# Packed attention and FFN on one core: FFN tiles of 384 tokens over pairs of batches, with the first pair in float32, in place of tiles of 288 tokens of one batch

## The chip, the cores and the metric

The kernel runs on one core of one Trainium2 chip. The metric is the device time of one execution in microseconds; lower is better. The kernel before took 830.7, 831.4 and 833.71 us in three runs, so the median is 831.4 us.

## What is computed

The reference, cut to what matters. There are 8 batches, 8 heads of 64 dimensions, 576 tokens per batch and 32 pack queries per head; the model width is 512 and d_ff is 2048.

```python
def sm_attn(qq, kk, vv):
    s = scale * qq @ kk.T
    a = exp(s - max(s)); a = a / (sum(a) + 1e-9)
    return a @ vv

p_packed = sm_attn(p, k, v)              # 32 x 64 per head
out = sm_attn(q, p_packed, p_packed)     # 576 x 64 per head
x = out, all heads side by side          # 4608 tokens x 512
h = x @ w_in                             # 4608 x 2048
g = maximum(h, 0) + alpha * minimum(h, 0)
y = g @ w_out                            # 4608 x 512
```

q, k, v, p and alpha are float32; w_in and w_out arrive as float64.

## The kernel before, in words

**Precision.** Most matmuls run in fp32r, a type whose matmul is one pass. To keep float32 accuracy an operand is split in two parts: hi is the operand cast to fp32r, lo is what is left (operand minus hi), and a product is three matmuls, hi·hi, hi·lo and lo·hi. A few parts run as plain float32 matmuls instead, without a split; the profile shows such a matmul as two records.

**Weights.** The float64 weights come in as raw 64-bit words, in blocks of 128 rows by 512 columns: 16 blocks of w_in and 16 of w_out. `convert` makes float32 of a block (ScalarE L117 and L119, VectorE L120, L123, L127 and L131) and splits it (ScalarE L133, VectorE L134). The split w_out stays on chip (`wo0` to `wo15`). The split w_in is used for the first batch at once and written to DRAM (`w_split`), from where later batches read it again.

**Attention.** The heads are handled in four pairs. `attention(b, tp)` does two pairs of one batch: scores of p against k, a softmax, transposes of its weights, a product with v (this gives the packed result), then scores of q against the packed result and a second softmax, whose weights end as `a_h` and `a_l` (split) or `a_f` (float32). The attention of batches 0 and 1 runs in float32 (`exact`): its scores are copied from PSUM to SBUF (L202, L204) before the softmax reads them. In later batches the score's hi and lo parts are added on VectorE (L211).

**Folding the packed result into w_in.** The second product of the attention, weights times packed result, is never made by itself. `packed_w` multiplies the packed result of a batch by w_in, three matmuls of 512 columns per block (L435 to L437), which gives `pw`; the FFN's first matmul is then attention weights times `pw`.

**The FFN.** It goes in steps. A step is one tile of 288 tokens (half a batch) and one block of 128 of the 2048 columns of d_ff; there are 16 tiles and 16 blocks, so 256 steps. `first(k, f)` makes h for the step in PSUM tile `ps_h`: six fp32r matmuls of 288 columns (L480 to L482, twice), or for batch 0 two float32 matmuls (L468). The leaky relu is `neg` on ScalarE (L486) and a multiply-add on VectorE (L487); then h is split into `gh` (ScalarE, L492) and `gl` (VectorE, L493). `second(k, f)` adds the step to four accumulators of 128 output columns each, with three matmuls of 288 columns per accumulator (L505 to L507). `split_pw` (L456, L458) splits `pw` for a tile before its steps need it.

**The order of the work.** One loop at the end of the program walks the 256 steps; at each step it also advances generators that do the rest, by the start steps in `plan`. The first 32 steps interleave the two tiles of batch 0 in blocks of four f, since the weights of a block come one by one; their partial sums are kept in `part` (L511, L518). The conversions of w_in and w_out advance one each in every second step of that stretch. `second` runs two steps behind `first`. From this program a scheduler writes a fixed order of instructions for each engine. SyncE issues all transfers in one queue, in its own order.

Of the kernel before, what the change touches and what calls it, by code (L numbers as in the profile page):

```python
# [15 lines left out]

# [12 lines left out]
def pack_attention_ffn_kernel(  # L29
# [13 lines left out]

# [19 lines left out]
    NG = S // 32  # L63

    const = ctx.enter_context(tc.tile_pool(name="const", bufs=1))
    xin = ctx.enter_context(tc.tile_pool(name="xin", bufs=3))
# [13 lines left out]

    w_split = dram.tile([NJ, NP, P, 2, 512], F32, name="w_split")


# [10 lines left out]
    s1f = const.tile([P, NP, 64], F32, name="s1f")  # L94
    p2f = const.tile([P, NP, 64], F32, name="p2f")
    pt0 = const.tile([P, NP, 2, 2, 64], F32R, name="pt0", tag=f"wo{NF - 1}")
    for t in (s1f, p2f, fv(s1), fv(p2), fv(pt0)):
        nc.gpsimd.memset(t, 0.0)
    wo_t = {}

    XF = 1

    def convert(src, raw, place):

# [10 lines left out]
        mag = xin.tile([P, 512], F32, name="mag", tag="xh")  # L115
        bits = mag.bitcast(U32)
        nc.scalar.activation(out=mag, in_=up, func=AF.Abs)  # L117
        low = xin.tile([P, 512], U32, name="low", tag="xl")
# [13 lines left out]
        hi, lo = place()  # L132
        nc.scalar.copy(out=hi, in_=mag)  # L133
        nc.vector.tensor_tensor(out=lo, in0=mag, in1=fv(hi), op=ALU.subtract)  # L134

    def new_raw(f=0):

        if f in left:
            left.remove(f)
            n = f  # L140
        elif f == NF - 1:
            n = f
        else:
            n = left.pop(0)
            left.append(n)
        return const.tile([P, 512], U64, name=f"wraw{n}", tag=f"wo{n}")

    SPARE = 4
    left = list(range(NF - 1 - SPARE, NF - 1))

    def load_w_out(f):
        def place():
            wo_t[f] = const.tile([P, 2, DM], F32R, name=f"wo{f}", tag=f"wo{f}")
            return wo_t[f][:, 0, :], wo_t[f][:, 1, :]

        raw = new_raw(f)
        convert(w_out[f * P : (f + 1) * P, :], raw, place)


    def load_x(src, b, pr):  # L160
        if b == 0 and (src is kT or pr == NP - 1):
            n = pr if src is kT else 2 * NP
            raw = const.tile([P, S], F32, name=f"xraw{n}", tag=f"wo{n}")
        else:
            raw = xin.tile([P, S], F32, name="xraw", tag="xraw", bufs=3)
        nc.sync.dma_start(out=raw, in_=src[b, pr])
        return raw
# [8 lines left out]
    def load_v(b, pr):  # L176
        if b == 0:
            raw = const.tile([P, KT, P], F32, name=f"vraw{pr}", tag=f"wo{NP + pr}")
        else:
            raw = vin.tile([P, KT, P], F32, name="vraw", tag="vraw")  # L180
        nc.gpsimd.memset(raw[: KT * P - S, KT - 1, :], 0.0)
        nc.sync.dma_start(
            out=raw[:, : KT - 1, :],
            in_=v[b, pr, : (KT - 1) * P].rearrange("(kt kp) d -> kp kt d", kp=P),
        )
        nc.sync.dma_start(out=raw[KT * P - S :, KT - 1, :], in_=v[b, pr, (KT - 1) * P :])
        return raw

    def scores(b, pr, st, x, dst, exact):

# [24 lines left out]
    def new_a(b):  # L215
        a_h = at.tile([P, 2, S], F32R, name="a_h", tag="a_h")
        a_l = at.tile([P, 2, S], F32R, name="a_l", tag="a_l", bufs=4)
        result[b] = (a_h, a_l)

    def attention(b, tp, exact=False):  # L220

# [48 lines left out]
        def split_v(i):  # L270
            if exact:
                return vraw[i]
# [361 lines left out]
```

## Time and profile before

| what | value |
|---|---|
| median of the three runs | 831.4 us |
| span of the profiled execution | 829.4 us |
| median minus span | 2.0 us |
| PE (matmul) busy | 784.3 us |
| VectorE (DVE) busy | 613.7 us |
| ScalarE (ACT) busy | 486.3 us |
| GpSimd (POOL) busy | 196.6 us |
| bytes moved | 97.97 MB |

The profile is of one execution. Its page gives the span, from the first to the last instruction; no time of the same execution beside the span is given, so the difference of 2.0 us between the runs' median and the span stands for what lies around it. PE is TensorE's matmul side and PEld its weight loads, which overlap. The matmuls are pipelined, so a record of a matmul lasts longer than the distance to the next one's start; it is the distance between starts that adds up to time. In a row of a group of instructions stand the line, the engine, the operation, output and input tiles, their shapes, the count; then busy time and the mean of one in ns; then the idle time of the engine before them and what ended it. In rows of windows stand the window, its length, and the busy time and count of each engine in the order PE, PEld, DVE, ACT, POOL, then the granted TensorE clock, the share of the DMA engines' time and GB/s.

### The profile page before, as it was taken

What the parts mean: (1) busy time and instruction counts of PE and PEld (TensorE: products, weight loads), DVE (VectorE), ACT (ScalarE), POOL (GpSimd) and SP (SyncE); (2) the same over time, 40 slices, a digit from 0 to 9 for tenths busy, and PEclk for the clock granted to TensorE, in tenths of its full rate; (3) what the DMA queues carried; (4) which work ended last, traced back from release to release, by engine and by line L of the source; (5) the groups of instructions that cost most, each with busy time, mean ns of one, the idle gap of its engine ahead of it and who ended that gap; (6) DMA issues with size and microseconds to landing.
All of it is one profiled execution on the core that took longest, in us unless ns stands there. A gap on an engine that the chain in (4) does not pass through costs nothing.

```text
span 829.4 us, 14959 instructions
## 1 busy us (share of the span) xinstructions
PE 784.3 (95%) x5384; PEld 730.6 (88%) x5384; DVE 613.7 (74%) x1311; ACT 486.3 (59%) x1141; POOL 196.6 (24%) x195
## 2 busy tenths in 40 slices
PE   5589989999999999999999999899999999999997
PEld 3348777798899989998999999889999999999997
DVE  4999999975777657889886587986955566666663
ACT  5778857756666775655567665655655433333332
POOL 2000012337666302353361024533210000000000
PEclk9779999999999999999999999999999999999999
DMA  9876846455523661322227532300252000000000
GB/s 304 279 249 224 291 166 232 151 180 168 202 90 109 223 203 33 101 59 72 61 76 247 186 87 58 100 15 16 88 196 91 14 30 2 29 1 29 5 27 29
DMA packets 55386, 97.97 MB, mean 118 GB/s; under 512 B 5136, under 2 KB 32784, under 8 KB 55312
## 3 DMA queue, kind: packets, MB, share of 16 engines
q1 hardware_dynamic: 55312, 97.02, 36.1%
q8 instruction: 42, 0.69, 0.3%
q14 instruction: 32, 0.26, 0.1%
HBM read 79.18 MB, written 17.83 MB: 117 GB/s over the span
## 4 chain that ended last, share of the span: by engine, by line
PE 73%; DVE 15%; DMA 5%; ACT 4%; issue 2%; POOL 0%; SPq 0%; ACTq 0%; DVEq 0%
PE acc L505 14%; PE acc L506 13%; PE acc L507 13%; PE ps_h L480 6%; PE ps_h L482 6%; PE ps_h L481 6%; PE ps_h L468 2%; PE ps_m L435 2%; DMA outT<-ot 1%; PE ps_m L436 1%; PE ps_m L437 1%; PE ps_m L316 1%; DVE ps_h L487 1%; DVE pwl L458 1%; DMA w<-w_split 1%
## 5 line engine op out<-in xcount | busy, mean ns | idle before, releaser
L505 PE MATMUL acc<-gh,wo 128*128 128x288 f32 x1024 | 288.6, 301 | 10.9 <-ACT gh L492 9.9
L506 PE MATMUL acc<-gh,wo 128*128 128x288 f32 x1024 | 282.6, 294 | 0.0
L505 PEld LDWEIGHTS acc<-gh,wo 128*128 128x128 f32 x1024 | 192.2, 188 | 22.3 <-ACT gh L492 15.2
L507 PE MATMUL acc<-gl,wo 128*128 128x288 f32 x1024 | 205.3, 300 | 0.0
L506 PEld LDWEIGHTS acc<-gh,wo 128*128 128x128 f32 x1024 | 192.3, 188 | 1.6
L492 ACT CAST gh<-ps_h 128x288 fp32r<-128x288 f32 x256 | 102.2, 400 | 124.1 <-DVE ps_h L487 114.8
L486 ACT ACTIVATE neg<-ps_h 128x288 f32<-128x288 f32 x256 | 105.4, 412 | 111.8 <-PE ps_h L482 102.6
L493 DVE TENSOR_TENSOR gl<-ps_h,gh 128x288 fp32r<-128x288 f32 x256 | 115.4, 452 | 73.4 <-ACT gh L492 72.4
L487 DVE SCALAR_TENSOR_TENSOR ps_h<-neg,nal,ps_h 128x288 f32<-128x288 f32 x256 | 132.0, 516 | 42.6 <-ACT neg L486 41.3
L507 PEld LDWEIGHTS acc<-gl,wo 128*128 128x128 f32 x1024 | 159.0, 188 | 3.7 <-issue 0.4
L480 PE MATMUL ps_h<-a_h,pwh 128*128 128x288 f32 x448 | 133.9, 299 | 1.1 <-DVE gl L493 0.6
L482 PE MATMUL ps_h<-a_h,pwl 128*128 128x288 f32 x448 | 131.8, 295 | 0.6 <-POOL pwl L458 0.6
L481 PE MATMUL ps_h<-a_l,pwh 128*128 128x288 f32 x448 | 131.9, 295 | 0.0
L173 POOL TENSOR_TENSOR xl<-xraw,xh 128x576 fp32r<-128x576 f32 x48 | 70.2, 1463 | 148.6 <-ACT xh L172 143.8
L480 PEld LDWEIGHTS ps_h<-a_h,pwh 128*128 128x128 f32 x448 | 84.1, 188 | 3.5 <-DVE gl L493 1.9
L482 PEld LDWEIGHTS ps_h<-a_h,pwl 128*128 128x128 f32 x448 | 83.9, 188 | 1.4 <-POOL pwl L458 1.1
L481 PEld LDWEIGHTS ps_h<-a_l,pwh 128*128 128x128 f32 x448 | 84.1, 188 | 0.4
L458 DVE TENSOR_TENSOR pwl<-pw,pwh 128x512 fp32r<-128x512 f32 x96 | 73.9, 770 | 7.1 <-PE ps_h L482 1.2
L456 DVE CAST pwh<-pw 128x512 fp32r<-128x512 f32 x112 | 56.0, 503 | 30.1 <-PE ps_h L481 28.6
L443 ACT COPY pw<-ps_m 64x512 f32<-64x512 f32 x112 | 65.0, 580 | 16.7 <-PE ps_m L437 12.7
L275 POOL TENSOR_TENSOR vs<-vraw,vs 128x640 fp32r<-128x640 f32 x24 | 38.6, 1609 | 42.7 <-ACT vs L274 42.2
L210 ACT COPY lo<-ps_m 64x288 f32<-64x288 f32 x96 | 37.8, 396 | 11.3 <-PE ps_m L208 9.8
(114 smaller groups left out, 1018.4 us busy)
## 6 DMA issues: line engine op xcount, KB each, us to landing
w<-w_split SPq DMA_DIRECT2D x64, 512.0 KB, 4.3
xraw<-in_kT SPq DMA_DIRECT2D x32, 288.0 KB, 2.9
xraw<-in_qT SPq DMA_DIRECT2D x32, 288.0 KB, 2.9
outT<-ot SPq DMA_DIRECT2D x64, 144.0 KB, 1.8
vraw<-in_v SPq DMA_DIRECT2D x32, 256.0 KB, 3.0
wraw<-in_w_out SPq DMA_DIRECT2D x16, 512.0 KB, 4.5
wraw<-in_w_in SPq DMA_DIRECT2D x16, 512.0 KB, 4.4
w_split<-w SPq DMA_DIRECT2D x16, 512.0 KB, 4.0
```

The source lines that it names most:

```text
L173: nc.gpsimd.tensor_tensor(out=xl, in0=raw, in1=fv(xh), op=ALU.subtract)
L458: eng.tensor_tensor(out=tl, in0=src, in1=fv(th), op=ALU.subtract)
L480: nc.tensor.matmul(ps[:, :HS], th[:, i, fs], a_h[:, i, tok], start=hi, stop=False)
L481: nc.tensor.matmul(ps[:, :HS], th[:, i, fs], a_l[:, i, tok], start=False, stop=False)
L482: nc.tensor.matmul(ps[:, :HS], tl[:, i, fs], a_h[:, i, tok], start=False, stop=lo)
L486: nc.scalar.activation(out=neg, in_=g, func=AF.Relu, scale=-1.0)
L487: nc.vector.scalar_tensor_tensor(out=g, in0=neg, scalar=nal[:, f : f + 1], in1=g, op0=ALU.mult, op1=ALU.add)
L492: nc.scalar.copy(out=gh, in_=g)
L493: nc.vector.tensor_tensor(out=gl, in0=g, in1=fv(gh), op=ALU.subtract)
L505: nc.tensor.matmul(acc[o][:, :HS], wo_t[f][:, 0, os_], gh, start=begin, stop=False)
L506: nc.tensor.matmul(acc[o][:, :HS], wo_t[f][:, 1, os_], gh, start=False, stop=False)
L507: nc.tensor.matmul(acc[o][:, :HS], wo_t[f][:, 0, os_], gl, start=False, stop=end)
```

## The change

The batches are taken in four groups of two. The 1152 tokens of a group form three FFN tiles of 384 tokens, so there are 12 tiles of 16 blocks, 192 steps. The middle tile has 192 tokens of each batch, and its `first` runs for the two batches apart, with matmuls of 192 columns.

The first group runs in float32 wherever the other groups split: attention (as before), the product of the packed result with w_in, and `first`, now for both batches. In its attention the scores of two head pairs go into one PSUM tile, by a stationary matrix of 128 columns with zeros in the other pair's place, and the maximum, the exponential and the transposes read PSUM directly, without the copies. w_in is multiplied as float32, written to DRAM as float32 (`w_whole`), read again later, split, and written as `w_split` for the other groups. The steps of the first group go in three sweeps over d_ff, blocks 0 to 3, 4 to 7 and 8 to 15, with all three tiles in each sweep; partial sums are kept in `part` between them. Of batch 1's attention the first half now runs ahead of the FFN.

The other groups run as before in fp32r, with 384 columns in `second` and in `first` of tiles 0 and 2. The lists `CONV`, `SWEEPS`, `starts` and `at_` set which step advances what. Several pools change their number of buffers. The core of the diff:

```diff
+    TS = 2 * S // 3
+    NT = 3
-    xin = ctx.enter_context(tc.tile_pool(name="xin", bufs=3))
-    at = ctx.enter_context(tc.tile_pool(name="at", bufs=3))
-    pwj = ctx.enter_context(tc.tile_pool(name="pwj", bufs=2))
-    win = ctx.enter_context(tc.tile_pool(name="win", bufs=3))
-    gp = ctx.enter_context(tc.tile_pool(name="gp", bufs=2))
-    op = ctx.enter_context(tc.tile_pool(name="op", bufs=2))
+    xin = ctx.enter_context(tc.tile_pool(name="xin", bufs=2))
+    at = ctx.enter_context(tc.tile_pool(name="at", bufs=7))
+    pwj = ctx.enter_context(tc.tile_pool(name="pwj", bufs=3))
+    win = ctx.enter_context(tc.tile_pool(name="win", bufs=2))
+    gp = ctx.enter_context(tc.tile_pool(name="gp", bufs=3))
+    op = ctx.enter_context(tc.tile_pool(name="op", bufs=4))
+    acc = ps_a.tile([P, NOC, 512], F32, name="acc")
...
+    def packed0(b, tp, k, vs):
+        ps2 = acc[:, 2 * tp : 2 * tp + 2, :HS]
+        for hf in range(2):
+            stair_scores(ps2[:, hf], s1f, k, tp, hf)
...
+        nc.vector.tensor_reduce(out=nmx, in_=ps2, axis=AX.XY, op=ALU.max, negate=True)
...
+    def packed_w0(j, pr, w):
...
+        nc.tensor.matmul(ps, ptf[:, pr], w, start=True, stop=True)
+        nc.sync.dma_start(out=w_whole[j, pr], in_=w)
...
+    def split_w_in(units):
+        for j, pr in units:
+            whole = pwj.tile([P, 512], F32, name="wf", tag="pwl")
+            nc.sync.dma_start(out=whole, in_=w_whole[j, pr])
+            w = win.tile([P, 2, 512], F32R, name="w", tag="w")
+            split_w(whole, w[:, 0, :], w[:, 1, :])
+            nc.sync.dma_start(out=w_split[j, pr], in_=fv(w))
...
-    def first(k, f):
+    def first(g, t, f):
+        for b, tok, at_ in pieces(g, t):
+            to = ps[:, at_]
+            if g == 0:
...
+                    nc.tensor.matmul(
+                        to, th[:, i, fs], a_f[:, i, tok], start=(i == 0), stop=(i == 1)
+                    )
+                continue
+            if (b, f // 2, t) not in pj:
+                split_pw(b, f // 2, t)
...
+            for i in range(2):
+                nc.tensor.matmul(to, th[:, i, fs], a_h[:, i, tok], start=(i == 0), stop=False)
+                nc.tensor.matmul(to, th[:, i, fs], a_l[:, i, tok], start=False, stop=False)
+                nc.tensor.matmul(to, tl[:, i, fs], a_h[:, i, tok], start=False, stop=(i == 1))
...
-    def second(k, f):
+    def second(g, t, f, sweep):
+        begin, end = f == sweep[0], f == sweep[1] - 1
+            ps, os_ = acc[:, o, :TS], slice(o * P, o * P + P)
...
+    SWEEPS = ((0, 4), (4, 8), (8, NF))
+    order = [(0, t, f, s) for s in SWEEPS for t in range(NT) for f in range(*s)]
+    order += [(g, t, f, (0, NF)) for g in range(1, B // 2) for t in range(NT) for f in range(NF)]
...
+    CONV = "ooioioioio--iiiiooiiiioo" + "-o-o-o-o"
```

In `CONV` a letter is one step of the loop: o converts a block of w_out, i one of w_in.

The order of instructions moves at two places of which the prediction speaks. The first is ScalarE at the start of the program. Before, this stood around the first exponential of batch 0's second softmax (L373): conversions (`mag`, `low`, `w`; `wraw` is a raw block of weights), score copies (`s`) of batch 0 and a cast for the attention of batch 1.

```order
L117 ACTIVATE mag<-wraw_380 128x512
L133 CAST w<-mag 128x512
L119 ACTIVATE low<-wraw_397 128x512
L202 COPY s_293<-acc_297 64x288
L243 CAST s_110<-praw 64x4x32 x2
L202 COPY s_293<-acc_305 64x288
L117 ACTIVATE mag<-wraw_397 128x512
L439 COPY pw<-ps_m 128x512
L373 ACTIVATE t_273<-t_273 128x576
```

After, this stands ahead of the same exponential, now L288. `wraw_444`, `wraw_457` and `wraw_478` are the first three raw blocks of w_out, and `aT` are the transposed weights of the first softmax of batch 1.

```order
L259 COPY p2f<-ps_m 64x2x32
L130 ACTIVATE low<-wraw_444 128x512
L244 COPY aT<-ps_m 128x384
L130 ACTIVATE low<-wraw_457 128x512
L244 COPY aT<-ps_m 128x256
L244 COPY aT<-ps_m 128x384
L244 COPY aT<-ps_m 128x256
L130 ACTIVATE low<-wraw_478 128x512
L288 ACTIVATE t_387<-t_387 128x576
```

So the first exponential of batch 0's second softmax now stands behind the first half of batch 1's attention, and behind reads of three blocks of w_out. On SyncE's queue those three loads stand behind all of k and v of both batches, four blocks of w_in and batch 0's q (before, the first block of w_out stood behind batch 0's k, v and q alone).

The second place is TensorE in a step of the FFN late in the program. Before, a step's `first` was six matmuls of 288 columns (`ps_h` is their PSUM tile, `a_h` and `a_l` the split attention weights, `pwh` and `pwl` the split `pw`):

```order
L480 MATMUL ps_h_10390<-a_h_7551,pwh_10361 128x288
L481 MATMUL ps_h_10390<-a_l_7552,pwh_10361 128x288
L482 MATMUL ps_h_10390<-a_h_7551,pwl_10362 128x288
L480 MATMUL ps_h_10390<-a_h_7551,pwh_10361 128x288
L481 MATMUL ps_h_10390<-a_l_7552,pwh_10361 128x288
L482 MATMUL ps_h_10390<-a_h_7551,pwl_10362 128x288
```

After, `first` of a step of the middle tile is twelve matmuls of 192 columns, six for each of the two batches (whose `a_h` have the numbers 5790 and 6642):

```order
L534 MATMUL ps_h_8025<-a_h_5790,pwh_7986 128x192
L535 MATMUL ps_h_8025<-a_l_5791,pwh_7986 128x192
L536 MATMUL ps_h_8025<-a_h_5790,pwl_7987 128x192
L534 MATMUL ps_h_8025<-a_h_5790,pwh_7986 128x192
L535 MATMUL ps_h_8025<-a_l_5791,pwh_7986 128x192
L536 MATMUL ps_h_8025<-a_h_5790,pwl_7987 128x192
L534 MATMUL ps_h_8025<-a_h_6642,pwh_7996 128x192
L535 MATMUL ps_h_8025<-a_l_6643,pwh_7996 128x192
L536 MATMUL ps_h_8025<-a_h_6642,pwl_7997 128x192
L534 MATMUL ps_h_8025<-a_h_6642,pwh_7996 128x192
L535 MATMUL ps_h_8025<-a_l_6643,pwh_7996 128x192
L536 MATMUL ps_h_8025<-a_h_6642,pwl_7997 128x192
```

Each step of tiles 0 and 2 has six such matmuls of 384 columns, and each step of every tile has twelve matmuls of 384 columns in `second`.

More of the change, by code (lines that the diff above doesn't have):

```diff
@@ L148, in pack_attention_ffn_kernel @@
[L148 to L157, printed above, removed]
-    def load_x(src, b, pr):
[L161 to L165, printed above, removed]
+        return mag
@@ new lines, in split_w, with load_w_out, w_out_steps, load_w_in @@
+    def split_w(src, hi, lo):
+        nc.scalar.copy(out=hi, in_=src)
+        nc.vector.tensor_tensor(out=lo, in0=src, in1=fv(hi), op=ALU.subtract)
+    def load_w_out(f):
+        mag = to_f32(w_out[f * P : (f + 1) * P, :], new_raw(f))
+        wo_t[f] = const.tile([P, 2, DM], F32R, name=f"wo{f}", tag=f"wo{f}")
+        split_w(mag, wo_t[f][:, 0, :], wo_t[f][:, 1, :])
+    def w_out_steps(fs):
+        for f in fs:
+            load_w_out(f)
+            yield
+    def load_w_in(j, pr):
+        return to_f32(w_in[pr * P : (pr + 1) * P, j * 512 : (j + 1) * 512], new_raw())
@@ new lines, in unpack0 @@
+    def unpack0(b, tp, q):
+        t1 = wk.tile([P, NG, 32], F32, name="t1", tag="w")
+        for hf in range(2):
+            if b:
+                ps = ps_m.tile([P, 512], F32, name="ps_m", tag="m")[:, :HS]
+            else:
+                ps = acc[:, 2 * tp + hf, :HS]
+            stair_scores(ps, p2f[b], q, tp, hf)
+            half = t1[:, hf * NG // 2 : (hf + 1) * NG // 2]
+            nc.vector.transpose(out=half.rearrange("p g n -> p (g n)"), in_=ps)
+        yield
+        yield from weights(b, tp, t1, nc.vector)
+        if b not in result:
+            result[b] = at.tile([P, 2, S], F32, name="a_f", tag="a")
+        nc.vector.transpose(out=result[b][:, tp, :], in_=t1.rearrange("p g n -> p (g n)"))
+        yield
@@ L496, in second @@
[L496 to L502 removed]
+        gh = gp.tile([P, TS], F32R, name="gh", tag="gh")
+        gl = gp.tile([P, TS], F32R, name="gl", tag="gl")
+        nc.scalar.copy(out=gh, in_=x)
@@ L586, in pack_attention_ffn_kernel @@
-    order = [(h, 4 * j + f) for j in range(NJ) for h in range(2) for f in range(4)]
-    order += [(k, f) for k in range(2, 2 * B) for f in range(NF)]
+    heads = [packed0(0, tp, k, vs) for tp in range(2)]
+    for _ in range(4):
+        for h in heads:
+            next(h)
+    praw, k = load_k0(1)
+    fill_s1f(praw)
+    w0 += [load_w_in(0, pr) for pr in range(2, NP)]
+    vs = load_v0(1)
+    q = load_q0(0)
+    heads = [packed0(1, tp, k, vs) for tp in range(2)]
+    for _ in range(4):
+        for h in heads:
+            next(h)
@@ new lines, in pack_attention_ffn_kernel, with add, converted @@
+    G = NT * NF
+    turns = {}
+    def add(gen, steps):
+        for at_ in steps:
+            turns.setdefault(at_, []).append(gen)
+        drains.append((steps[-1], gen))
+    drains = []
+    wi = packed_w0_steps(units(1, 2, 3))
+    def converted(what):
+        for ch in what:
+            if ch != "-":
+                next(wo if ch == "o" else wi)
+            yield
+    CONV = "ooioioioio--iiiiooiiiioo" + "-o-o-o-o"
+    add(converted(CONV), range(len(CONV)))
+    for tp in range(2):
+        add(unpack0(1, tp, q), [0, 0, 1, 1, 2])
@@ L588, in pack_attention_ffn_kernel @@
     AHEAD = 2
     for i in range(len(order) + AHEAD):
-        now = [gen for t, gen, n in plan for _ in range(max(1, -n)) if t <= i and (n < 0 or (i - t) % n == 0)]
+        now = turns.get(i, [])
         for gen in now[0::2]:
```

543 lines of the change are left out of this document (262 added, 281 removed).

## The prediction

> **What bounds the kernel now.** I read the page first, for the engines' shares and their course over the span (40 slices of 20.7 us, each digit a share in tenths).
>
> ```profile
> span 829.4 us, 14959 instructions
> PE 784.3 (95%) x5384; PEld 730.6 (88%) x5384; DVE 613.7 (74%) x1311; ACT 486.3 (59%) x1141; POOL 196.6 (24%) x195
> PE   5589989999999999999999999899999999999997
> DVE  4999999975777657889886587986955566666663
> L505 PE MATMUL acc<-gh,wo 128*128 128x288 f32 x1024 | 288.6, 301 | 10.9 <-ACT gh L492 9.9
> ```
>
> PE is full from about the tenth slice on; before that VectorE is. The last conversion of a weight marks the change, so I cut the windows there, and once more at the first L487, which is the first step of the FFN.
>
> ```profile
> 53.30 0.52 DVE L487 SCALAR_TENSOR_TENSOR ps_h<-neg,nal,ps_h 128x288 f32<-128x288 f32 x1
> 160.18 0.68 DVE L134 TENSOR_TENSOR wo<-mag,wo 128x512 fp32r<-128x512 f32 x1
> 0.00:53.30 53.30, 33.29 (x119) 19.58 (x119) 40.99 (x89) 34.84 (x77) 4.35 (x19) 0.78 0.83 275
> 53.30:160.80 107.50, 101.17 (x563) 80.97 (x563) 104.20 (x224) 81.47 (x187) 13.12 (x13) 1.00 0.67 227
> 160.80:829.40 668.60, 649.88 (x4706) 630.02 (x4704) 468.55 (x1002) 369.99 (x878) 179.13 (x163) 1.00 0.28 88
> ```
>
> Three stretches, then. Up to 53.3 us the inputs arrive and attention runs in a chain; VectorE idles 53.3 - 41.0 = 12.3 us. Up to 160.8 us VectorE works 104.2 of 107.5 us (idle 3.3). After it PE works 649.9 of 668.6 us. So the time is VectorE's work up to the last conversion, plus its idle time there, plus PE's work that is left then.
>
> **The change part by part: PE.** The price of a matmul is the distance between starts. Two L480 with three steps of 18 matmuls between them, and the first and last of three matmuls of 512 columns:
>
> ```profile
> 700.90 0.30 PE L480 MATMUL ps_h<-a_h,pwh 128*128 128x288 f32 x1
> 708.05 0.30 PE L480 MATMUL ps_h<-a_h,pwh 128*128 128x288 f32 x1
> 291.61 0.39 PE L435 MATMUL ps_m<-w,pt 128*128 128x512 f32 x1
> 292.07 0.40 PE L437 MATMUL ps_m<-w,pt 128*128 128x512 f32 x1
> ```
>
> 7.15 us / 54 = 132.4 ns for 288 columns, and 0.46 / 2 = 230 ns for 512. The line through both is 0.436 ns per column and about 7 ns fixed. No row shows 384; the line gives 174.2 ns, with 172.5 (512's price per column) and 176.5 (288's) as bounds. No row shows 192 either; the line gives 90.6 ns. But each matmul has its weight load, and there are rows of loads one after another:
>
> ```profile
> 87.90 0.52 PEld L338 LDWEIGHTS ps_m<-ii,c 64*128 64x128 f32 x4 [0.17 <-ACT low L119]
> 59.35 0.97 PE ps_h L468 x4
> L507 PEld LDWEIGHTS acc<-gl,wo 128*128 128x128 f32 x1024 | 159.0, 188 | 3.7 <-issue 0.4
> ```
>
> Four loads take 0.52 us with the last one lasting some 0.19, as the L507 row has it, so they start (0.52 - 0.19) / 3 = 0.11 us apart. I take 111 ns for a matmul of 192 columns, since its load has nothing longer to hide behind; the bounds are 90.6 (hidden) and 132.4 (a matmul of 288). In float32 four records, two matmuls of 288, take 0.97 us, so 485 ns per matmul.
>
> The sums: `second` is 3072 x 132.4 = 406.7 us before, 2304 x 174.2 = 401.4 after (-5.3). fp32r `first` is 1344 x 132.4 = 177.9, and becomes 576 x 174.2 + 576 x 111 = 164.3 (-13.6). Float32 `first` doubles with batch 1: 64 x 485 = 31.0 becomes 62.1 (+31.1). The product with w_in is 240 x 230 = 55.2, and becomes 144 x 230 plus 16 float32 matmuls of 485 x 512 / 288 = 862 ns, 46.9 (-8.3). In the first group's attention the 40 products with v move 64 columns for 128, at most 40 x 485 x 64 / 288 = -4.3 us, nothing if loads set their pace: -1.6. In all PE's work changes by +2.3 us: what tiles of 384 save, the float32 `first` of batch 1 takes back.
>
> The Trainium skill (TensorE: Matmul & The Clock Gate, Back-to-back issue gap) gives another slope, 81 ns per sustained matmul at 128 columns and 131 at 512, by which 384 columns would cost little more than 288; the rows above disagree, 132.4 at 288 and 230 at 512, and I keep their line.
>
> **VectorE up to the last conversion.** The groups of VectorE in the window up to 160.8 us:
>
> ```profile
> L131 DVE CUSTOM_DVE_ANT_0 mag<-mag,low 128x1024 uint16<-128x1024 uint16 x32 | 22.7, 709 | 0.0
> L487 DVE SCALAR_TENSOR_TENSOR ps_h<-neg,nal,ps_h 128x288 f32<-128x288 f32 x28 | 14.4, 513 | 0.0
> L493 DVE TENSOR_TENSOR gl<-ps_h,gh 128x288 fp32r<-128x288 f32 x27 | 12.1, 448 | 1.1 <-ACT gh L492 1.0
> L134 DVE TENSOR_TENSOR wo<-mag,wo 128x512 fp32r<-128x512 f32 x16 | 10.8, 678 | 0.2
> L518 DVE TENSOR_TENSOR part<-acc,part 128x288 f32<-128x288 f32 x16 | 6.5, 445 | 0.7 <-PE acc L507 0.7
> L369 DVE TENSOR_REDUCE m<-t 128x18 f32<-128x576 f32 x4 | 3.0, 746 | 0.0
> L355 DVE TENSOR_TENSOR pt<-p2f,pt 128x64 fp32r<-128x64 f32 x8 | 2.6, 371 | 0.2 <-ACT pt L354 0.2
> L211 DVE TENSOR_TENSOR s_t<-ps_m,lo 64x288 f32<-64x288 f32 x6 | 2.6, 444 | 0.1
> L204 DVE COPY s_t<-acc 64x288 f32<-64x288 f32 x4 | 1.8, 448 | 4.3 <-PE acc L200 4.3
> L244 DVE TENSOR_TENSOR s<-praw,s 64x128 fp32r<-64x128 f32 x2 | 0.6, 286 | 0.1
> ```
>
> The 32 conversions stay, five instructions each. By the order of the changed program, the last split of w_out has 28 FFN steps ahead of it on VectorE, as the 28 of L487 show for before. These are a third wider: from 445 ns at 288 columns to 678 at 512 is about 1.02 ns per column, so 98 ns more for each of 55 instructions, +5.4 us. Partial sums: 18 instructions of 543 ns for 16 of 445, +2.7 us. The rest is attention, of which more stands ahead, since the next group's starts at step 3: 16 more score additions of 444 ns (+7.1), six more reduces of 746 (+4.5), 3.6 us of transposes, some 35 small ones at the 286 ns of L244 (+9.8); gone are eight score copies of 448 and eight splits of 371 (-6.6). That is +18.4, and +26.5 in all.
>
> Instructions on VectorE overlap: all durations in the window (count times mean over its groups) sum to 169.1 us, but the busy time there is 41.0 + 104.2 = 145.2, a factor of 0.859. So it becomes (169.1 + 26.5) x 0.859 = 168.0 us.
>
> **The start.** What arrives when:
>
> ```profile
> 0.00:10.00 10.00, 4.66 (x14) 2.45 (x15) 2.88 (x4) 2.73 (x6) 4.35 (x19) 1.00 0.78 241
> 10.00:20.00 10.00, 6.84 (x38) 5.39 (x36) 5.16 (x16) 7.79 (x19) 0.00 (x0) 0.83 1.04 364
> 20.00:30.00 10.00, 9.25 (x48) 5.85 (x47) 9.78 (x23) 9.84 (x29) 0.00 (x0) 1.00 0.97 327
> wraw<-in_w_out SPq DMA_DIRECT2D x16, 512.0 KB, 4.5
> w<-w_split SPq DMA_DIRECT2D x64, 512.0 KB, 4.3
> L373 ACT ACTIVATE t<-t x2: 683/685/687, 31.0 to 38.9; 128x576 f32<-128x576 f32 x2
> ```
>
> The DMAs bring 2.4 + 3.6 + 3.3 = 9.3 MB in 30 us. In the new order 20 inputs of 288 KB, four blocks of 512 KB and two small ones, 8.1 MB, stand on SyncE's queue ahead of w_out's first block; with its first three and three writes of `w_whole` it is 10.4 MB, the last byte at 30 + 1.1 / 0.327 = 33.4 us. ScalarE's exponential of batch 0's second softmax now stands behind reads of all three blocks, so it starts at about 35 us; before it started at 31.0, and the first L487 came 22.3 us later. I take the same distance: the FFN starts at 57.3 us. VectorE has 42.5 us of durations ahead of that by the new order; before it had 47.2 for 41.0 busy, so 36.8 busy and 57.3 - 36.8 = 20.5 idle. With 3.3 idle behind, the last conversion ends at 168.0 + 20.5 + 3.3 = 191.8 us.
>
> **What PE has left then.** Up to its last conversion PE now does more: the same 28 steps with float32 `first` at 4/3 of 0.97 us (+9.0), 336 matmuls of `second` (+14.0), the w_in product in float32 (16 x 862 for 48 x 230 ns, +2.8), 32 more score matmuls less what the products with v save (+2.6): 28.4 us. So 668.6 + 2.3 - 28.4 = 642.5 us are left. In the L505 row PE waits 9.9 us for `gh`; the chain behind it grows by a fifth (L487: 513 to 611 ns), a step by a third, so I take 5 us off (bounds 0 and 9.9). Span: 191.8 + 642.5 - 5 = 829.3. The median stands 2.0 over the span of before, so the forecast is 831.
>
> **Edits at no cost.** The trip of w_in through `w_whole` adds 8.4 MB; in the stretch in which it falls the DMAs are busy 0.67 of the time; at 327 GB/s it is 26 us of their time, which the idle third holds. If it doesn't, late inputs hold VectorE, up to 26 us. Two `win` buffers for three: a block takes 4.3 us, one is used per step of at least 12 x 174 + 6 x 174 ns = 3.1 us, and two are ahead; without that cover PE waits 1.2 us per block. Splitting `pw` three times per block falls on VectorE behind 160.8 us, where it is busy 468.6 of 668.6 us.
>
> **Rivals.** First, slower: the start hangs on the first three blocks of w_out. If they come at the rate of the first window, 241 GB/s, 10.4 MB take 43 us, the exponential comes at 44 and the FFN starts at 66: +8.7, 840 us. It decides from a start of 62 us (831 + 4.7). For it speaks ScalarE's order; against it the 364 and 327 GB/s.
>
> Second, slower: VectorE overlaps less with fewer conversions between chains of softmax. Over the whole span the page's 613.7 busy stand against 679 of durations, 0.904; then 195.6 x 0.904 = 176.8, +8.8, 840 us.
>
> Third, faster: the start is no later. If idle time stays at 12.3, the FFN starts at 49 us: -8.2, 823 us. For it: the score copies and splits go, the exponential reads PSUM, and four L204 had waited 4.3 us. Against it: half of batch 1's attention now comes first.
>
> Fourth, faster: 192 columns at 90.6 ns. 576 x 20.4 ns = -11.8, 819 us. For it: in FFN steps PEld runs ahead of PE; against it the 0.11 us between loads.
>
> Fifth, faster: a matmul's price is mostly fixed. By the rows the lower bound of 384 columns is 1.7 ns under the line, 2880 x 1.7 = -5 us, 826. By the Trainium skill's slope in the section named above, as an estimate, 384 columns would take 145 ns and the time would fall to about 750; no row bears that out.
>
> **How the numbers follow.** The measurement can tell about 0.5% from no change, 827.2 to 835.6 us. The forecast, 831, has 0.28. The slower rivals have 0.22 and 0.12, the faster ones 0.20, 0.14 and 0.04. So faster 0.38, same 0.28, slower 0.34. Both signs hold most of the chance; the forecast's own range is 827 to 836, from the bounds of `gh` (5 either way). The whole range adds the third and fourth cases below (831 - 8.2 - 11.8 = 811, taken as 812) and the first and second above (831 + 8.7 + 8.8 = 848).
>
> **What would show it.** The first L540 at 57 us (rivals: 49 or 66); the last split of w_out at 192 us; 111 ns between starts of L534 to L536 in the middle tile, 174 in L554 to L556; PE full behind the last conversion with under 15 us idle. It is wrong if PE waits there for DMA or for VectorE, which no row of before shows, or if VectorE isn't full between 57 and 192 us.

## The result

The changed kernel takes 878.9 us (median of four runs), the kernel before 832.6 us in the same series: a ratio of 1.055 with a 95% interval of 1.050 to 1.059. The forecast was 831 us with a range of 812 to 848; it is 48 us off. The page of the changed kernel:

```profile
span 873.8 us, 12763 instructions
PE 795.0 (91%) x4472; PEld 727.1 (83%) x4472; DVE 593.5 (68%) x1157; ACT 463.8 (53%) x973; POOL 181.0 (21%) x178
L554 PE MATMUL acc<-gh,wo 128*128 128x384 f32 x768 | 271.5, 354 | 32.3 <-ACT gh L545 9.1
```

VectorE and ScalarE have less to do than before, PE hardly more, and yet the span is 44 us longer. PE's idle time ahead of L554, the first matmul of an output block, is 32.3 us, where the same line before (L505) had 10.9. To place the loss, both programs are cut at the first step, at the middle and at the end of the first two batches' FFN. Before:

```profile
0.00:52.20 52.20, 32.19 (x116) 19.39 (x117) 39.89 (x86) 33.74 (x74) 4.35 (x19) 0.78 0.82 272
52.20:176.30 124.10, 117.47 (x662) 94.79 (x661) 116.99 (x253) 91.92 (x214) 20.34 (x19) 1.00 0.64 215
176.30:286.80 110.50, 106.75 (x749) 100.12 (x747) 78.00 (x171) 74.79 (x175) 65.12 (x60) 1.00 0.50 160
286.80:829.40 542.60, 527.93 (x3863) 516.26 (x3861) 378.86 (x804) 285.86 (x682) 106.79 (x97) 1.00 0.23 72
```

After:

```profile
0.00:57.00 57.00, 39.78 (x178) 27.91 (x179) 36.17 (x81) 36.18 (x75) 10.84 (x28) 0.94 0.89 292
57.00:203.20 146.20, 115.55 (x502) 91.36 (x501) 127.60 (x250) 101.43 (x204) 30.38 (x26) 0.89 0.55 183
203.20:307.50 104.30, 99.25 (x517) 87.05 (x517) 63.62 (x127) 59.15 (x125) 27.86 (x26) 1.00 0.49 156
307.50:873.80 566.30, 540.39 (x3281) 520.77 (x3279) 366.12 (x701) 267.06 (x571) 111.91 (x98) 1.00 0.21 67
```

Some 21 us are lost by the end of the first two batches (307.5 for 286.8), and 24 in the six batches behind them (566.3 for 542.6), where PE is idle or waiting for 25.9 us, before 14.7. Of the other 12 of these 24 us, some 8 are an estimate from the prediction's prices: in these six batches `second` has 4.0 us less of matmuls and `first`, with its 192 columns, 11.8 more. In the first half of the first two batches PE's granted clock (third figure from the end of a row) is 0.89, before 1.00.

The prices of the matmuls came out as forecast. In the timeline of PE in the last group, the first and last rows of 21 matmuls of 384 columns, and of 11 of 192:

```profile
766.23 0.33 PE L554 MATMUL acc<-gh,wo 128*128 128x384 f32 x1
769.70 0.33 PE L556 MATMUL acc<-gl,wo 128*128 128x384 f32 x1
769.96 0.28 PE L535 MATMUL ps_h<-a_l,pwh 128*128 128x192 f32 x1
771.08 0.27 PE L536 MATMUL ps_h<-a_h,pwl 128*128 128x192 f32 x1
```

3.47 / 20 = 173.5 ns (forecast 174.2) and 1.12 / 10 = 112 ns (forecast 111). So these prices are not the loss. Just ahead of these rows, at the end of a tile, the timeline of all engines shows waits:

```profile
760.08 0.55 DVE L572 COPY ot<-acc 128x384 f32<-128x384 f32 x1
...
760.68 0.45 PE L554 MATMUL acc<-gh,wo 128*128 128x384 f32 x1 [0.22 <-DVE ot L572]
...
761.56 0.48 ACT L570 COPY ot<-acc 128x384 f32<-128x384 f32 x1
...
762.10 0.44 PE L554 MATMUL acc<-gh,wo 128*128 128x384 f32 x1 [0.62 <-ACT ot L570]
...
762.98 0.56 DVE L572 COPY ot<-acc 128x384 f32<-128x384 f32 x1 [0.73 <-PE acc L556]
...
764.04 0.36 PE L554 MATMUL acc<-gh,wo 128*128 128x384 f32 x1
...
765.05 0.50 ACT L570 COPY ot<-acc 128x384 f32<-128x384 f32 x1
...
765.60 0.44 PE L554 MATMUL acc<-gh,wo 128*128 128x384 f32 x1 [0.85 <-ACT ot L570]
```

Copies out of PSUM and matmuls alternate: every L554 but the one at 764.04, which has rows of `first` ahead of it, waits for a copy, and the copy at 762.98 for a matmul. Four copies of half a microsecond stand in a row, for which PE did not wait before (its waits are shown with e2). My first reading was that this is the wait of the next tile for its accumulators; e9 and e10 below show what it is.

### The profile page after: what moved, and what is told of

It is laid out like the page before. It is cut to its first block, busy times and chain, and to the rows that moved or that the text cites. A ratio compares the mean times of both kernels' runs of the same rounds, so it can differ in the third digit from the quotient of the medians.

```text
span 873.8 us, 12763 instructions
## 1 busy us (share of the span) xinstructions
PE 795.0 (91%) x4472; PEld 727.1 (83%) x4472; DVE 593.5 (68%) x1157; ACT 463.8 (53%) x973; POOL 181.0 (21%) x178
## 4 chain that ended last, share of the span: by engine, by line
PE 66%; DVE 19%; DMA 5%; ACT 5%; issue 4%; POOL 0%; SPq 0%; ACTq 0%; DVEq 0%; POOLq 0%
PE acc L554 13%; PE acc L556 12%; PE acc L555 12%; PE ps_h L534 5%; PE ps_h L535 5%; PE ps_h L536 5%; PE ps_h L524 4%; DMA w<-w_split 2%; DVE ps_h L540 2%; DVE pwl L513 2%; DMA wf<-w_whole 2%; DVE mag L138 2%; DVE pwh L512 1%; PE ps_m L418 1%; DVE mag L142 1%
## 5 line engine op out<-in xcount | busy, mean ns | idle before, releaser
L554 PE MATMUL acc<-gh,wo 128*128 128x384 f32 x768 | 271.5, 354 | 32.3 <-ACT gh L545 9.1
L556 PE MATMUL acc<-gl,wo 128*128 128x384 f32 x768 | 263.3, 343 | 0.0
L555 PE MATMUL acc<-gh,wo 128*128 128x384 f32 x768 | 261.0, 340 | 0.0
L554 PEld LDWEIGHTS acc<-gh,wo 128*128 128x128 f32 x768 | 146.2, 190 | 46.7 <-ACT gh L545 11.2
L540 DVE SCALAR_TENSOR_TENSOR ps_h<-neg,nal,ps_h 128x384 f32<-128x384 f32 x192 | 117.4, 614 | 77.3 <-ACT neg L539 76.4
L545 ACT CAST gh<-ps_h 128x384 fp32r<-128x384 f32 x192 | 91.9, 479 | 142.2 <-DVE ps_h L540 123.4
L539 ACT ACTIVATE neg<-ps_h 128x384 f32<-128x384 f32 x192 | 94.2, 492 | 121.8 <-PE ps_h L536 103.6
L546 DVE TENSOR_TENSOR gl<-ps_h,gh 128x384 fp32r<-128x384 f32 x192 | 105.7, 551 | 71.4 <-ACT gh L545 70.8
L555 PEld LDWEIGHTS acc<-gh,wo 128*128 128x128 f32 x768 | 146.2, 190 | 3.9 <-issue 0.5
L534 PE MATMUL ps_h<-a_h,pwh 128*128 128x384 f32 (+1 forms) x384 | 117.2, 305 | 2.0 <-DVE gl L546 1.6
L536 PE MATMUL ps_h<-a_h,pwl 128*128 128x384 f32 (+1 forms) x384 | 116.9, 304 | 0.6 <-DVE pwl L513 0.6
L535 PE MATMUL ps_h<-a_l,pwh 128*128 128x384 f32 (+1 forms) x384 | 117.0, 305 | 0.0
L524 PE MATMUL ps_h<-a_f,pw 128*128 128x384 f32 (+1 forms) x256 | 74.8, 419 | 10.5 <-DVE gl L546 7.8
L490 ACT COPY pw<-ps_m 64x512 f32<-64x512 f32 x96 | 55.8, 581 | 25.9 <-PE ps_m L487 24.3
```

What stands on the lines that cost most here:

```text
L524: nc.tensor.matmul(to, th[:, i, fs], a_f[:, i, tok], start=(i == 0), stop=(i == 1))
L534: nc.tensor.matmul(to, th[:, i, fs], a_h[:, i, tok], start=(i == 0), stop=False)
L535: nc.tensor.matmul(to, th[:, i, fs], a_l[:, i, tok], start=False, stop=False)
L536: nc.tensor.matmul(to, tl[:, i, fs], a_h[:, i, tok], start=False, stop=(i == 1))
L539: nc.scalar.activation(out=neg, in_=x, func=AF.Relu, scale=-1.0)
L540: nc.vector.scalar_tensor_tensor(out=x, in0=neg, scalar=nal[:, f : f + 1], in1=x, op0=ALU.mult, op1=ALU.add)
```

## The experiments

The theories: A, the trip of w_in through DRAM; B, the ends of tiles and sweeps; C, the next group's attention comes too early; D, GpSimd slows VectorE; E and F, the width of the tiles or the grouping; G, two buffers for blocks of w_in; H, the accumulators as one tile; I, two buffers for split k and q. In e5, e11, e12 and e15 tiles have 288 tokens, in e6 and e10 the kernel before is changed, in the others the changed kernel. e2, e4, e8 and e13 leave out a part of the result.

**e1, the trip through DRAM.** In `packed_w0`:

```diff
-        nc.sync.dma_start(out=w_whole[j, pr], in_=w)
+        ws = win.tile([P, 2, 512], F32R, name="w", tag="w")
+        split_w(w, ws[:, 0, :], ws[:, 1, :])
+        nc.sync.dma_start(out=w_split[j, pr], in_=fv(ws))
...
-    add(split_w_in(units(*range(NJ))), [16 + n for n in range(16)])
```

> w_in is split from the converted block at once and written as hi and lo; the float32 copy in DRAM and its reading back are gone, and nothing else changes. Theory A (the trip through DRAM holds ScalarE's queue, and behind it VectorE, while the weights are converted): VectorE's idle time between the first step of the FFN and the last split of w_out, 19.7 us in the changed kernel, falls under 9 us, and the time falls by 11 to 20 us, to 859 to 868. Theories B (evictions), C (the second group's attention comes too early) and D (GpSimd lengthens VectorE's instructions): within 4 us of the changed kernel's 879.

877.9 us, 1.0 less. Theory A falls, although the chain of waits showed transfers of `wf` in it: what they held up was late anyway.

**e2, copies that don't read the accumulators.** In `second`, three times like this:

```diff
-                nc.scalar.copy(out=to, in_=ps)
+                nc.scalar.copy(out=to, in_=fixed)
```

> Every copy or addition that takes an accumulator out of PSUM reads a constant tile in SBUF in its place, so the engines have the same instructions, but PE never waits for an accumulator to be read before it starts the next tile or sweep; the output is left out by that. Theory B (PE waits at the 18 ends of tiles and sweeps for the accumulators): each end costs about 2.2 us by the distances between steps in the last group, so the time falls by 15 to 35 us, to 844 to 864, and the idle time ahead of L554 falls from 32 us to under 15. Theories A, C and D: within 5 us of 879.

880.8 us. By this, B would fall. But the waits of PE in the six later batches show that one wait took the place of the other. The longest two of the kernel before, then those of the changed kernel:

```profile
PE acc L505 <- ACT gh L492: 6.0, 7, 2.2
PE ps_m L435 <- DMA w<-w_split: 1.2, 2, 1.0
```

```profile
PE acc L554 <- ACT ot L570: 6.0, 9, 1.0
PE ps_m L485 <- DMA w<-w_split: 4.6, 4, 1.5
PE acc L554 <- DVE ot L572: 1.8, 4, 0.7
```

And e2:

```profile
PE ps_m L487 <- DMA w<-w_split: 8.9, 6, 2.4
```

PE now waits for the blocks of w_in (L487 of e2 is L485 of the changed kernel). The six later batches take 565.2 us, for 566.3 in the changed kernel. The first group ends 9.9 us later in the profiled execution (317.4 for 307.5); why stays open. That made theory G.

**e3, a later attention.**

```diff
-        starts = (3, 6, 16, 19) if g == 1 else (0, 3, 15, 18)
+        starts = (18, 21, 29, 32) if g == 1 else (0, 3, 15, 18)
...
+        if g == 1:
+            at_ = [42] + [44 + n for n in range(16)]
```

> The attention of the second group starts at steps 18, 21, 29 and 32 in place of 3, 6, 16 and 19, and its product with w_in follows at step 42. Nothing is left out. Theory C (this attention loads VectorE in the stretch that VectorE bounds): the last split of w_out comes at 190 to 200 us in place of 220, and most of that stays, 855 to 868 us. If the stretch is bound by the chain of steps and transfers (A) the last split comes by less than 10 us sooner and the time stays within 6 us of 879 or rises, since the attention then falls into the stretch that PE bounds.

898.9 us, 20 slower. The splits of w_out, in the changed kernel and in e3 (first to last):

```profile
L147 DVE TENSOR_TENSOR wo<-mag,wo x13: 671/680/1718, 68.0 to 219.2; 128x512 fp32r<-128x512 f32 x13
```

```profile
L147 DVE TENSOR_TENSOR wo<-mag,wo x14: 681/686/693, 59.6 to 166.4; 128x512 fp32r<-128x512 f32 x14
```

The last split comes 53 us sooner, and the time rises. So C is wrong, and the last conversion does not mark what my sum took it for: in the changed kernel it moves with the order of the work, not with what bounds it.

**e4, no splits on GpSimd** for the second group: `split_x` and `split_v` return a kept tile of zeros as the lo part for batches 2 and 3.

```diff
+        if b < 4:
+            nc.scalar.copy(out=xh, in_=raw)
+            return xh, kept["xl"]
```

> In the second group's attention the lo parts of k, q and v are tiles of zeros, so GpSimd's splits of them are left out (L333, L388, some 26 us of its time beside the conversions). Theory D (VectorE's instructions last longer where GpSimd works beside them: 848 ns for 679 of L138, 950 for 682 of L147): VectorE's busy time between the first step and the last split of w_out falls by 6 to 9 us, and the time by as much, 870 to 873. Theories A to C: within 4 us of 879.

872.6 us, 6.3 less, as D expected. In the profiled executions the last split ends 6.5 us sooner (214.0 for 220.5), and more than half of that is lost again behind it (spans of 870.9 and 873.8). VectorE up to the last split, the changed kernel from 60 us on and then e4 from 55.7 us on:

```profile
L138 DVE SCALAR_TENSOR_TENSOR mag<-wraw,mag 128x512 uint32<-128x512 uint32 x24 | 19.3, 805 | 0.1
L147 DVE TENSOR_TENSOR w<-wf,w 128x512 fp32r<-128x512 f32 x16 | 13.0, 819 | 3.9 <-ACT w L146 3.9
```

```profile
L138 DVE SCALAR_TENSOR_TENSOR mag<-wraw,mag 128x512 uint32<-128x512 uint32 x25 | 17.2, 688 | 0.1
L147 DVE TENSOR_TENSOR w<-wf,w 128x512 fp32r<-128x512 f32 x16 | 10.9, 688 | 10.9 <-ACT w L146 10.5 <-DMA xraw<-in_kT 0.4
```

The same instructions last 805 and 819 ns on average beside GpSimd's splits, 688 without. The Trainium skill (GPSIMD Engine Reference, 1. Specifications) says that GpSimd shares its interfaces to SBUF with VectorE and collides there with instructions that have two inputs in SBUF or run in a two-port mode. Both lines have two inputs, and for them the trace agrees. It does not for L142, which has two (`mag` and `low`) and lasted 694 ns at most in the same stretch of the changed kernel. L131 and L134, with one input, reached 1512 and 1755 ns; no row shows the mode they ran in.

**e5, tiles of 288 tokens.**

```diff
-    TS = 2 * S // 3
-    NT = 3
+    TS = S // 2
+    NT = 4
...
+        steps = [at_ * 4 // 3 for at_ in steps]
```

> The changed kernel with tiles of 288 tokens, four to a group of two batches, so no tile has tokens of two batches and no matmul has 192 columns; all lists of steps are stretched by 4/3. Nothing is left out. By the prices of matmuls alone PE has 6.5 us less (second +5.3, first of groups 2 to 4 -11.8). Theory E (the wide tiles are the cause: longer chains from step to step and longer ends of tiles): the time falls to 835 to 855 us. Theory F (the grouping is the cause: two batches in float32 beside the conversions, partial sums, the order of the attention): it stays at 866 to 882.

902.5 us: neither. It is 24 us slower, and it has 24 ends of tiles and sweeps for 18 (its copies and additions out of the accumulators are 96 for 72, four to an end; the 28 of e11's expectation is a slip). Whatever an end costs, narrow tiles pay it more often, so B was not dead.

**e6, the kernel before with both first batches in float32 `first`.**

```diff
-    XF = 1
+    XF = 2
```

> The kernel before, with first in float32 for batches 0 and 1 in place of batch 0 alone, and nothing else. Nothing is left out. PE has 32 steps of 0.97 us for 0.794, +5.6 us, VectorE and GpSimd lose the splits of batch 1's product with w_in. If float32 costs what its matmuls cost, 834 to 841 us. If it is a main cause of the slower time through waits, over 846.

838.8 us for 832.1 (ratio 1.0096, 1.0068 to 1.0125): +6.7, about the 5.6 of its matmuls. Float32 is not the cause.

**e7 and e8, three buffers for blocks of w_in,** in e8 with copies as in e2 (read from a block of w_out). The buffers are paid for elsewhere:

```diff
-    win = ctx.enter_context(tc.tile_pool(name="win", bufs=2))
-    op = ctx.enter_context(tc.tile_pool(name="op", bufs=4))
+    win = ctx.enter_context(tc.tile_pool(name="win", bufs=3))
+    op = ctx.enter_context(tc.tile_pool(name="op", bufs=2))
```

> The changed kernel with three buffers for blocks of w_in as before the change, paid for with two buffers of the output tiles and one each of two small tiles. Nothing is left out. Theory G (two buffers make PE wait for blocks of w_in in the later groups, 5.6 us ahead of L485): the wait falls under 2 us and the time by 3 to 6 us, to 873 to 876. Otherwise within 3 us of 879.

> As e7, and what takes an accumulator out of PSUM reads a block of w_out in SBUF in its place, so that PE never waits for it; the output is left out by that. Theory B (the ends of tiles) with G: in e2 the wait for ends became one for blocks of w_in, which three buffers take away, so now the time falls by 10 to 16 us, to 863 to 869. If neither matters, within 5 us of 879.

e7 takes 884.7 us, 5.8 more; e8 872.2, 12.4 less than e7. Between kernels with the same buffers, the copies' hold on PE is worth 12 us. Both missed what was expected: e7 rose where G had 3 to 6 us less, and e8 is 6.6 us under the changed kernel where 10 to 16 were expected. G alone looked wrong, and e14 will correct that.

**e9 and e10, four accumulators or one.** The order of the changed program, PE in the last step of a tile and the first of the next (`wo_2276` is the last block of w_out, `wo_454` the first; rows of `first` left out), shows on whom the matmuls wait:

```
L554 MATMUL acc<-gh,wo_2276 128x384 [waits DVE_49]
L555 MATMUL acc<-gh,wo_2276 128x384
L556 MATMUL acc<-gl,wo_2276 128x384
L554 MATMUL acc<-gh,wo_2276 128x384 [waits Activation_49]
L555 MATMUL acc<-gh,wo_2276 128x384
L556 MATMUL acc<-gl,wo_2276 128x384
...
L554 MATMUL acc<-gh,wo_2276 128x384 [waits DVE_49]
L555 MATMUL acc<-gh,wo_2276 128x384
L556 MATMUL acc<-gl,wo_2276 128x384
L554 MATMUL acc<-gh,wo_454 128x384 [waits Activation_49]
```

The waits are inside the last step of the old tile. Its output block 1 waits for VectorE, block 2 for ScalarE, block 3 for VectorE: each for the copy of the block before it. They read and write different columns, but `acc` is now one tile, and a write to one part waits for the reads of another. e9 gives the changed kernel four tiles again (the first group's scores have a pool of their own, closed before the FFN); e10 gives the kernel before one:

```diff
-    acc = ps_a.tile([P, NOC, 512], F32, name="acc")
+    start = ExitStack()
+    ps_s = start.enter_context(tc.tile_pool(name="ps_s", bufs=1, space=bass.MemoryType.PSUM))
+    pair = [ps_s.tile([P, 2, 512], F32, name=f"pair{n}", tag=f"pair{n}") for n in range(2)]
...
+        if begin:
+            acc[:] = [ps_a.tile([P, 512], F32, name=f"acc{o}", tag=f"acc{o}") for o in range(NOC)]
```

```diff
+    acc_all = ps_a.tile([P, NOC, 512], F32, name="acc")
...
-                    tag = f"acc{(2 * pr + hf) % 4}"
-                    ps = ps_a.tile([P, 512], F32, name=tag, tag=tag)
+                    ps = acc_all[:, (2 * pr + hf) % 4, :]
...
-            acc[:] = [ps_a.tile([P, 512], F32, name=f"acc{o}", tag=f"acc{o}") for o in range(NOC)]
+            acc[:] = [acc_all[:, o, :] for o in range(NOC)]
```

> The changed kernel with four accumulator tiles as before the change; the scores of the first group's first softmax, which need two banks in one tile, have a pool of their own, closed before the FFN. Nothing is left out. Theory H (since the accumulators are one tile of four banks, the matmuls of output block 1 in the last step of a tile wait until block 0 is copied out, block 2 until block 1 is, and so on: four copies in a chain at each of 18 ends): the wait of PE at the ends goes, the idle time ahead of L554 falls from 32 us to under 15, the last group (175.8 us) falls by 8 to 11 us, and the time by 20 to 35 us, to 844 to 859. If the ends cost because wide copies are slow (B without H), it stays within 6 us of 879.

> The kernel before with its four accumulators made one tile of four banks, and nothing else. Nothing is left out. Theory H: each of its 22 ends of tiles and partial sums gets a chain of four copies, 2 to 3 us each in the 14 ends where PE bounds, so the time rises by 25 to 50 us, to 857 to 882, and PE's idle time ahead of L505 rises from 11 us to over 30. If one tile does not matter: within 4 us of 832.

e9 takes 859.2 us, 19.7 less (just under the 20 to 35 expected). The last group falls by 9.6 us (166.2 for 175.8), as expected; PE's idle time ahead of the first matmul of an output block falls to 18.7 us, where under 15 was expected. e10 takes 885.9 us for 831.9 (ratio 1.065, 1.063 to 1.068), 54 more, beyond the 25 to 50 expected: the one edit makes the kernel before slower than the changed one. PE's idle time ahead of L505 is 18.5 us, for 10.9 before, where over 30 was expected; so the time does not all stand as idle time ahead of that line. PE's waits in e10's last group of two batches, where the kernel before had none:

```profile
PE acc L505 <- ACT ot L522: 5.4, 9, 0.8
PE acc L505 <- DVE ot L524: 1.2, 2, 0.6
```

And e10's first L487 rows, which in the kernel before begin at 53.30:

```profile
L487 DVE SCALAR_TENSOR_TENSOR ps_h<-neg,nal,ps_h x6: 504/510/521, 71.0 to 89.2; 128x288 f32<-128x288 f32 x6
```

Some 18 of its 54 us come before the FFN. The first softmax's scores share the tile too, and PE waits there 5.9 us for copies of scores (L200 on L202 and L204), before none; the rest of the 18 is not traced. That the one tile is slower (theory H) is shown both ways.

**e11 and e12, narrow tiles without the chain of copies:** e9 with the edit of e5; e12 has three buffers in the pool of split k and q.

```diff
-    xin = ctx.enter_context(tc.tile_pool(name="xin", bufs=2))
+    xin = ctx.enter_context(tc.tile_pool(name="xin", bufs=3))
```

> e9 (four accumulators) with tiles of 288 tokens as in e5. Nothing is left out. In e5 tiles of 288 made it 24 us slower; theory H says that this was ten more chains of copies, since there are 28 ends for 18. Without the chains only the prices of matmuls are left, 6.5 us in favour of 288, so 848 to 858 us where e9 took 859. If narrow tiles have another cost, over 865. If wide tiles are what is left of the slower time, 832 to 842.

> e11 with three buffers in the pool of split k and q as before the change, for two. Nothing is left out. Theory I (two buffers hold GpSimd's splits until the scores have read them, SyncE's queue waits behind, and blocks of w_in come late): PE's wait for blocks of w_in and for the later groups' attention shrinks, the time falls by 4 to 12 us against e11. Otherwise within 4 us of e11.

e11 takes 838.3 us (median of ten runs, 832.8 to 842.8), 20.9 less than e9, where the prices of matmuls give 6.5. e12 takes 834.9, 3.4 less than e11, within the 4 us that count as nothing for I. So without the chain wide tiles cost 14 us that their matmuls don't explain.

**e13, e9 with the edits of e1 and e4.**

> e9 with the edits of e1 (w_in split at once, no trip through DRAM) and e4 (lo parts of k, q and v of the second group are zeros, GpSimd's splits of them left out). With the chain of copies gone, A and D should add up: D took 6.3 us in e4; A alone took nothing in e1, but in e9 ScalarE still waits 10.1 us for the trip between the first step and step 24, so 845 to 853 us. If A stays without effect, 851 to 855.

856.7 us, 2.5 less than e9 and above both expectations: with the chain gone, A and D together are small. D's 6.3 us are not a fixed price.

**e14 and e15.** e14 is e9 with the buffers of e7; e15 is e12 with the edit of e1.

> e9 with three buffers for blocks of w_in (as in e7, paid for with two buffers of output tiles and one each of two small tiles). Nothing is left out. If two buffers are why the wide tiles cost more than their matmuls (PE waits 5.8 us for blocks in e9's later groups, none in e11's), the time falls by 4 to 8 us, to 851 to 855. If not, it stays within 4 us of 859 or rises, since two output buffers make the copies wait for the transfers out.

> e12 (288 tokens, four accumulators, three buffers for split k and q) with w_in split at once as in e1. Nothing is left out. e12 took 835 where the kernel before took 832. If the trip through DRAM still holds ScalarE in the first group, 826 to 832; if not, 833 to 837. A version under both kernels needs less than 831.

e14 takes 841.9 us (ratio to before 1.012, 1.010 to 1.014), 17.3 less than e9, where 4 to 8 were expected. The six later batches, e9 and then e14:

```profile
296.70:857.10 560.40, 540.70 (x3281) 529.12 (x3280) 349.26 (x700) 279.15 (x587) 108.42 (x98) 0.98 0.23 74
```

```profile
295.30:838.60 543.30, 531.71 (x3278) 521.65 (x3276) 355.48 (x702) 275.51 (x585) 107.64 (x98) 1.00 0.24 76
```

All 17 us are there: 8 are PE's idle time (19.7 us in e9, 11.6 in e14), and 9 are busy time for the same matmuls (540.7 and 531.7). The waits of PE in this stretch, e9 and then e14:

```profile
PE acc L558 <- ACT gh L547: 7.3, 5, 2.2
PE ps_m L487 <- DMA w<-w_split: 5.8, 5, 1.8
PE ps_h L536 <- DVE pwh L514: 2.3, 2, 1.1
```

```profile
PE ps_m L487 <- DMA w<-w_split: 2.9, 3, 1.4
PE acc L558 <- ACT gh L547: 1.1, 1, 1.1
```

The wait for blocks halves. That the longer waits for `gh` and `pwh` followed from the late blocks fits, but is argued; e14 also has two output buffers for four, and which buffers count was not tried one by one.

The longer busy time goes with the granted clock, 0.98 in e9's row and 1.00 in e14's. One of e9's waits for `gh`, and PE shortly after it (window, length, busy time and count, clock, DMA share, GB/s):

```profile
423.59 0.44 PE L558 MATMUL acc<-gh,wo 128*128 128x384 f32 x1 [2.24 <-ACT gh L547]
425.00:428.00 3.00, 3.00 (x13) 0.50 0.02 5
```

Behind a gap of 2.24 us the clock is 0.50 for some 3 us, in which matmuls of 384 columns start 0.32 us apart, for 0.174 at full clock. Summed over windows of 1 us, the time that the clock is short of full (length times one minus clock) is 10.5 us in e9's six later batches and 0.9 in e14's. So by this sum a wait there costs about as much again by the slow clock behind it.

With the chain of copies, the same edit had cost 5.8 us (e7). Narrow tiles (e11) do without the third buffer: there PE has no wait for a block in this stretch. So e14's 17 us and e11's 14 are largely one cost, of two buffers together with wide tiles, and are not to be added; both edits in one kernel were not run. e15 takes 836.9 us, so the trip through DRAM has no effect there either. Of the variants none beats the kernel before; e12 is nearest, at a ratio of 1.0039 (1.002 to 1.0059).

## Why the prediction was wrong

**The prices of fp32r matmuls: right.** 173.5 and 112 ns for 174.2 and 111. PE's sum (+2.3) can't be read off by itself, since waits and the clock lengthen the busy time: +10.7 us in the changed kernel, +0.8 in e14 (785.1 for 784.3). The fourth rival (192 columns at 90.6) is excluded, and of the fifth the 145 ns; its bound by rows, 172.5, is within 1 ns of what was measured. The Trainium skill's 131 ns for 512 sustained columns (TensorE: Matmul & The Clock Gate, Back-to-back issue gap) does not hold for this stream, which takes 173.5 at 384.

**The start: right within 3 us, in part by luck.** By the first rows of L540, forecast 57 us:

```profile
L540 DVE SCALAR_TENSOR_TENSOR ps_h<-neg,nal,ps_h x6: 602/604/604, 60.0 to 88.6; 128x384 f32<-128x384 f32 x6
```

The first rival (66 us) and the third (49) did not come. The exponential began at 35.5 us (forecast about 35), and the first L540 came 24.4 us later (22.3 was taken over). But what the exponential was to wait for did not hold it: between 20 and 36 us ScalarE waits 3.8 us for PE's transposes and packed products, 1.0 for a block of w_in, and none for w_out's blocks stands among its waits.

**"The last conversion ends at 191.8 us": wrong,** it is 220.5. Worse, the cut itself failed. The changed kernel in the prediction's three stretches:

```profile
0.00:60.00 60.00, 40.57 (x180) 28.19 (x180) 39.17 (x88) 37.72 (x78) 10.84 (x28) 0.94 0.85 277
60.00:220.50 160.50, 128.53 (x565) 102.00 (x566) 140.85 (x277) 111.05 (x224) 34.78 (x29) 0.90 0.59 198
220.50:873.80 653.30, 625.87 (x3729) 596.91 (x3727) 413.48 (x795) 315.04 (x672) 135.36 (x121) 1.00 0.24 76
```

Before, VectorE worked 104.2 of 107.5 us in the second stretch; now it works 140.9 of 160.5, so it was no longer full, which the prediction had named as what would make it wrong. In the sum's own terms, the span is 44.5 us over the forecast 829.3. VectorE's idle time in the second stretch, taken over as 3.3 us, is 19.7 (+16.4); its busy time up to the last conversion is 180.0 us for 168.0 (+12.0); the idle time of the start is as forecast (+0.3); and what follows takes 653.3 us for 637.5 (+15.8). There PE is idle for 27.4 us, where under 15 was named. e3 moved the last split by 53 us without a gain.

**"Edits at no cost": the step that failed.** It named the trip through DRAM (rightly at nothing: e1, e15) and two `win` buffers, priced at nothing by a cover of two loads ahead. It did not name the accumulator tile at all. I had read the line that makes `acc` one tile of four accumulators as a matter of layout. Its price: 19.7 us here (e9), 54 in the kernel before (e10). The `win` buffers, with what else e14 changes, cost 17.3 us more once the chain is gone; the bound that I gave, 1.2 us per block for 48 blocks, is above that, but the range did not take it in, and the waits for blocks themselves are the smaller part (5.8 us in e9, 2.9 in e14). It also said that no row of before shows PE waiting for DMA or VectorE behind the last conversion. That is a misreading: PE waits there 1.2 us for blocks of w_in and 0.6 for `gl`, so the cover was not complete even with three buffers.

**"I take 5 us off" for `gh`: not borne out.** The wait for `gh` ahead of L554 is 9.1 us, for 9.9 before, and PE's slack in the six later batches grew from 14.7 to 25.9 us. With the four accumulators and e14's buffers that growth is gone: e14 has 543.3 us there for 542.6 before, with PE idle 11.6 us.

**What is left.** The forecast of 831 and the result of 879 differ by 48: 20 for the one tile, 17 for the buffers, 11 that e14 (842) still has. By its windows most of those lie in the first group, which ends at 295.3 us for 286.8 before, 8.5 later:

```profile
55.40:176.60 121.20, 103.86 (x490) 85.39 (x490) 106.33 (x215) 83.34 (x167) 22.24 (x19) 0.94 0.57 186
176.60:295.30 118.70, 107.79 (x536) 92.91 (x535) 87.69 (x169) 73.93 (x154) 35.76 (x33) 0.94 0.48 158
```

No engine is full in either window: neither VectorE (106.3 of 121.2) nor PE (107.8 of 118.7). PE's granted clock is 0.94 in both, in the kernel before 1.00; 6% of the 240 us is some 14 us, an estimate of what PE loses by it, so the slow clock behind waits could be the whole 8.5 us. That is argued: no run changes it alone. What the waits come from stays open too. Without GpSimd's splits and the trip of w_in e9 took at most 2.5 us less (e13). The order of the first group's steps is where I would look, and it was not tried alone.

**The rivals.** All but the second were about the start and the prices. The second (VectorE slower up to its last conversion, since its instructions overlap less) had the right place and was right in part. Up to 220.5 us VectorE's durations (count times mean over its groups) sum to 201.1 us and its busy time is 180.0, a factor of 0.895, where the sum took 0.859 and the rival 0.904. (By this count the sum's 169.1 is 167.7, a factor of 0.866, which leaves its 168.0 as it is.) Of the 12.0 us of busy time above, about half is this factor and half the longer durations. The 16.4 us of waiting are in no rival. No rival was a wait added by how buffers are declared, though the diff showed three such edits.

## What to carry to other kernels

When a diff merges several tiles into one or changes the number of a pool's buffers, look at the waits in the new order of instructions at the places where such a tile is released and taken again, before pricing the arithmetic: a tile is the unit of dependence, and four accumulators in one tile, copied out in turn, become a chain. Test two suspected waits together as well as apart: removing one showed nothing (e2) or even a loss (e7) while the other stood behind it. Look at the granted clock behind a wait before pricing the wait by its length alone. A cut of the time at an event (here the last conversion) is good only as long as what ends there bounds the time.

## What the runs showed of the hardware

Some of VectorE's instructions lasted far longer beside GpSimd's splits: the splits of w_out have a median of 680 ns and a longest of 1718 in the changed kernel, and 693 as the longest in e3, where GpSimd's splits came later. One L131, of 418 ns in the median, took 1.51 us from 92.09 us on, while a split on GpSimd ran from 91.92 us for 1.40. What leaving these splits out gained was 6.3 us in e4 and, with the chain of copies gone and w_in split at once, 2.5 in e13.

PE's granted clock fell to 0.50 behind a gap: in e9 behind one of 2.24 us, for some 3 us, in which matmuls of 384 columns started 0.32 us apart, for 0.174 at full clock.
